# One written order for the transform units over all 376 steps, and B units on 128 rows

## The chip, the cores and the metric

The kernel runs on one core of a Trainium2 chip. The time is the device time in microseconds (us) of one execution; the time before is the median of three runs. Beside it there is one execution taken by the hardware profiler, whose instructions, queues and waits the profile page and the trace show. All durations below are from that execution.

## The reference, cut to what matters

```python
# x: (8, 3008, 256) float32; w_r, w_i: (256, 256); b_r, b_i: (256,)
X  = rfft(x, axis=1)
Yr = X.real @ w_r - X.imag @ w_i + b_r
Yi = X.real @ w_i + X.imag @ w_r + b_i
Yr, Yi = (sign(Y) * max(abs(Y) - 0.01, 0) for Y in (Yr, Yi))
y  = irfft(Yr + 1j * Yi, n=3008, axis=1)         # (8, 3008, 256)
h  = y.reshape(24064, 256) @ moe_w_in            # w_in: (256, 2048)
g  = where(h > 0, h, exp(min(h, 0)) - 1)         # ELU
out = g @ moe_w_out                              # w_out: (2048, 256), out: (24064, 256)
```

A Fourier transform along the sequence, a complex matrix product with a soft threshold in the frequency domain, the transform back, and then a two-layer network with ELU on each of the 24064 tokens.

## The kernel before

**The network** is cut into 376 steps. Tokens go in 47 blocks of 512, and each block takes eight steps; in step i, `front(i)` makes two 128-wide slices of h for one block (four matmuls with 512 columns, L1006; where the block crosses from one batch into the next each is split in two pieces), ScalarE takes the exponential, and a VectorE instruction (L1048, or L1050) joins it with h into `gT`. `back(i - 2)` multiplies the `gT` of two steps before with w_out (eight matmuls with 256 columns, L1080) into the sums of the block. Every eighth step the sums are copied to `osb` and stored.

The result of `front` lies in PSUM in a pool `psH` of two buffers, so `front(i + 1)` can begin only when the VectorE instruction of step i - 1 has read its `hps`. That instruction is put on VectorE by `finish_elu()` in the step after its own, behind whatever that step's unit puts on VectorE. A step has one of three ways to make the ELU:

- "pool": ScalarE makes two exponentials of 128x512, GpSimd a minimum and maximum of each (L1059), VectorE two instructions of 128x512.
- "act": ScalarE makes a ReLU and an exponential of 128x1024 (L1024, L1025), VectorE one instruction of 128x1024; GpSimd does nothing.
- otherwise: one exponential, then two VectorE instructions of 128x1024 (L1061, L1050). The first batch's steps use it.

**The transform** is cut into units, each put ahead of a step's `front`, so that TensorE does it between the step's matmuls. One batch has 6 units A (first stage of the transform, then a store to DRAM), 8 units X (second stage, after `load_Z` has brought the first one back from DRAM with its axes turned), 12 units M (`unit_M(b, q, i)`, the complex product with bias and threshold), 6 units B (`unit_B(b, q)`, first stage back, from the two M units of one q, then a store to DRAM) and 8 units Y (`unit_Y`, second stage back, after `load_Bs` has brought the B units' result back). Y units 0 and 1 make the first quarter of a batch's tokens, 2 and 3 the second, and so on.

A unit M makes six matmuls with 256 columns (L289, from batch 2 on; from the sum `XS` of real and imaginary part, made on GpSimd by `sum_XT`, L224). VectorE copies one product (L144) and adds it to the others (L296); GpSimd adds the bias (L301), clips (L302) and subtracts (L303) into the tile `Y`. A unit B takes `Y` as it lies, 64 rows for each of two halves s, with the real and the imaginary part c added up in PSUM: two pp times two c times two s, eight matmuls on 64 rows with 256 columns (L375).

The units share one PSUM buffer of two banks, or for M two buffers of one bank in the same place. `XT` and `Z` have one buffer each.

**The order** was made for each batch of 47 steps by `plan(b)`: M units stood in runs of two, three or four with a Y or B unit between the runs, and the X units of a batch came after the first Y units of the batch before. Steps with a unit M and a few more were in "act", other steps with units in "pool". Y units in an "act" step are read out by VectorE (L144), else by ScalarE (L146). The two Y units 0 and 1 of the next batch, "n" in the plan, stood at the end.

SyncE's queue carries, in the program's order, the loads and stores of A, X and B and the stores of the output; GpSimd's queue carries the loads of x. An instruction that waits holds up what is behind it on its queue.

The last lines of `unit_B` and the call of `finish_elu` in the loop are what the change and the steps below turn on:

```python
        for pp in range(2):
            for c in range(2):
                for s in range(2):
                    nc.tensor.matmul(
                        ps[:, s, pp * D : pp * D + D],
                        lhsT=M3[s * N2 : s * N2 + N2, 2 * v + pp, c, :],
                        rhs=Y[s * N2 : s * N2 + N2, pp, c * D : c * D + D],
```

Of the kernel before, what the change touches and what calls it, by code (L numbers as in the profile page):

```python
# [20 lines left out]
N2 = 64  # L21
# [8 lines left out]
def kernel(  # L30
# [28 lines left out]
    M3 = constp.tile([P, K1 // 2, 2, P], BF16, name="M3")  # L59
# [6 lines left out]
    bias_p = constp.tile([P, 2 * D], BF16, name="bias_p")  # L66
# [10 lines left out]
    space = constp.tile([P, 384], BF16, name="space")  # L77
# [26 lines left out]
    Y_of = {}  # L104
    Bz_of = {}
# [122 lines left out]
    def sum_of(dt, ch):  # L228

        return XS[:, 3 * dt + ch] if 3 * dt + ch < 5 else busy[:]  # L230

# [8 lines left out]
    def m_group(b, q, i, ps, biased=False):  # L240
# [10 lines left out]
        if i == 0:  # L251
            Y_of[b, q] = wk3.tile([P, 2, 2 * D], BF16, name="Y", tag="Y")
# [11 lines left out]
    def unit_M(b, q, i):  # L264
# [8 lines left out]
        if i == 0:  # L273
            Y_of[b, q] = wk3.tile([P, 2, 2 * D], BF16, name="Y", tag="Y")
# [10 lines left out]
        if o == 0 and b > 3:  # L285
            todo.append(todo.pop(0))
# [76 lines left out]

    def unit_B(b, v, alone=False, on_dve=False, all_dve=False):
# [5 lines left out]
        Bz, Y = Bz_of[b, v // 2], Y_of.pop((b, v))  # L370
        ps = unit_ps("bps", alone)
        for pp in range(2):
            for c in range(2):
                for s in range(2):
                    nc.tensor.matmul(  # L375
                        ps[:, s, pp * D : pp * D + D],
                        lhsT=M3[s * N2 : s * N2 + N2, 2 * v + pp, c, :],
                        rhs=Y[s * N2 : s * N2 + N2, pp, c * D : c * D + D],
                        start=(c == 0), stop=(c == 1),
                    )  # L380
# [33 lines left out]
    def split_B(v, ps, on_dve=(False, True), by_half=False):  # L414
# [8 lines left out]
        def half(pp):  # L423
            for c in range(2):
                for s in range(2):
                    nc.tensor.matmul(
                        ps[s][:, pp * D : pp * D + D],
                        lhsT=M3[s * N2 : s * N2 + N2, 2 * v + pp, c, :],
                        rhs=Y[s * N2 : s * N2 + N2, pp, c * D : c * D + D],
                        start=(c == 0), stop=(c == 1),  # L430
                    )
# [22 lines left out]
    def turn_B(v, ts=(0, 1), ps=None, on_dve=False):  # L454
# [11 lines left out]
        for pp in range(2):  # L466
            for dt in ts:
                for c in range(2):
                    for s in range(2):
# [7 lines left out]
                            rhs=M3[s * N2 : s * N2 + N2, 2 * v + pp, c, :].rearrange(  # L477
# [76 lines left out]

    nc.vector.memset(bias_p[:], 0.0)
# [274 lines left out]
    XS = sump.tile([P, 5, 512], BF16, name="XS")  # L830
# [60 lines left out]
    for o, src, sc, bi in ((1, w3, TURN, 0.0), (0, a3, -TURN, hpi[:])):  # L891
        if o == 0:
            nc.scalar.activation(a3[:], w3[:], AF.Abs)
        nc.scalar.activation(
            M3[:, :, 0, o * N2 : o * N2 + N2], src[:], AF.Sin, bias=bi, scale=sc
        )
# [3 lines left out]
        M3[:, :, 1, 0:N2], M3[:, :, 0, N2:P], 2.0, sgb, ALU.mult, ALU.mult  # L900
    )
    nc.vector.scalar_tensor_tensor(
        M3[:, :, 1, N2:P], M3[:, :, 0, 0:N2], -2.0, sgb, ALU.mult, ALU.mult
# [150 lines left out]
    def elu(i, hps, Et, on_pool, on_act):  # L1054
# [7 lines left out]
        late_elu.append((i, hps, Et, on_pool or on_act, on_pool))  # L1062
# [44 lines left out]
    def put(kind, b, *a):  # L1107
        return ({"A": unit_A, "X": unit_X, "M": unit_M, "B": unit_B, "Y": unit_Y}[kind], (b, *a))

    def plan(b):  # L1110

        f0 = [[] for _ in range(PER)]
        f1 = [[] for _ in range(PER)]
        mode = [None] * PER
        n1, n2 = b + 1, b + 2
        mid = [("X", u) for u in range(8)] + [
# [4 lines left out]
        ]  # L1121
        if n1 < B:
            if b:
                lead, xs = 0, (3, 6, 9) if b < 3 else (3, 8, 13)

                def M(q):
                    return [("M", q, 0), ("M", q, 1)]

                shift = b - 1 if b < 3 else b - 3
                seq = [("y", 2), ("y", 3)] + [None] * shift + [("X", u) for u in range(8)]  # L1130
                if b < 3:
                    seq += [("y", 4)] + M(0) + M(1) + [("y", 5), ("B", 0)]
                else:
                    seq += M(0) + [("y", 4)] + M(1) + [("y", 5), ("B", 0)]
                seq += M(2) + [("y", 6), ("B", 1)] + M(3) + [("y", 7), ("B", 2)]
                on_act = [("X", 4), ("X", 7), ("B", 3)] + [("y", u) for u in range(5, 8)]
                if b < 3:
                    on_act += [("A", 0)]
                    seq += M(4) + [("B", 3)] + M(5) + [("A", 0), ("B", 4), ("B", 5)]
                    seq += [("A", u) for u in range(1, 6)]  # L1140
                else:
                    on_act += [("y", 4), ("B", 4)]
                    seq += M(4) + [("B", 3), ("A", 0)] + M(5) + [("B", 4), ("A", 1), ("B", 5)]
                    seq += [("A", u) for u in range(2, 6)] + [None] * (3 if n2 == B else 2)
                seq += [("n", 0), ("n", 1)]
            else:
                lead, seq = FILL, (
                    [u for u in mid if u[0] != "A"]
                    + [("A", 0), ("A", 1), ("A", 2), ("n", 0), ("n", 1)]
                    + [("A", u) for u in range(3, 6)]  # L1150
                )
                xs = (12, 15, 18)
        else:
            lead, seq = 0, [("y", u) for u in range(2, 8)]
        for t, u in enumerate(seq, lead):
            if u is None:
                continue
            if b and n1 < B:
                mode[t] = "act" if u in on_act or u[0] == "M" else "pool"
            if mode[t] == "act" and u[0] != "M":  # L1160
                k = {"y": "Y"}.get(u[0], u[0])
                c = {"y": b, "A": n2}.get(u[0], n1)
                if c < B:
                    dve = (False, True) if k == "B" else (k != "X" or b < 3 and u[1] == 7,)
                    f0[t].append(put(k, c, u[1], False, *dve))
            elif u[0] == "y":
                f0[t].append(put("Y", b, u[1]))
            elif u[0] == "n":
                f0[t].append(put("Y", n1, u[1]))
            elif u[0] == "A":  # L1170
                if n2 < B:
                    f0[t].append(put("A", n2, u[1]))
            else:
                f0[t].append(put(u[0], n1, *u[1:]))
            if u == ("B", 5):
                f1[t + (b > 0 and n2 < B)] += [
                    (load_Bs, (n1, w, 0, 4 * K1 - 16 * (b == w == 0))) for w in range(4)
                ]
            if u == ("A", 5) and n2 < B:
                cuts = (0, 8, NS) if b else (0, 8, 16, 24, NS)  # L1180
                f1[t] += [(load_Z, (n2, *part)) for part in zip(cuts, cuts[1:])]
        if b == 0:
            for t in range(6):
                f1[t].append((unit_A, (1, t, False, t not in (0, 2), True)))
            for t, a, u in (
                (7, f0, 2), (7, f1, 3), (8, f0, 4), (8, f1, 5), (9, f0, 6), (9, f1, 7)
            ):
                a[t].append((split_Y, (0, u)))
            f1[1].insert(0, (scale_w_in, (1, True, 1)))
            for w in range(1, 4):  # L1190
                f1[w].append((load_Bs, (0, w)))
            f1[5] += [(load_Z, (1, s0, s1)) for s0, s1 in ((0, 8), (8, 16), (16, NS))]
            f1[xs[0]].append((lambda: gate(Z_of[1][:, 16, 0:1]), ()))
        if n2 < B:
            for ci in range(3):
                f1[xs[ci]].append((load_x, (n2, ci)))
        if b and n1 < B:
            f0[seq.index(("X", 4))].append((sum_XT, (n1, 0)))
            f0[seq.index(("X", 7))].append((sum_XT, (n1, 1, range(2 if b < 3 else 3))))
            if b < 3:  # L1200
                f0[seq.index(("M", 2, 0))].insert(0, (sum_XT, (n1, 1, (2,))))
        return f0, f1, mode

    f0 = f1 = None
    bare = 0
    early_h = None
    for i in range(n + LAG):
# [11 lines left out]
        elif i < n:  # L1219
            r = i % PER  # L1220
            if r == 0:
                f0, f1, mode = plan(i // PER)
                used = [bool(u0 or u1) for u0, u1 in zip(f0, f1)]
            free = not used[r]
            bare = bare + 1 if free else 0
            calm = free and (i >= n - 2 or (r + 2 < PER and not used[r + 1] and not used[r + 2]))
            for f, a in f0[r]:
                f(*a)
# [60 lines left out]
```

## Time and profile before

| | |
|---|---|
| time, median of three runs | 893.57 us (893.43 to 893.65) |
| span of the profiled execution | 903.9 us, from its first to its last instruction |
| TensorE busy | 891.3 us (99%) |
| VectorE, ScalarE, GpSimd busy | 679.6, 722.4, 596.7 us |
| granted TensorE clock | 0.948 on the mean; 0.95 in each of the stretches of 100 us from 100 to 800 us |
| units B (L375) | 336 matmuls on 64 rows, 42 units |
| DMA engines' share, 100 to 700 us | 0.39 to 0.42 |

A step is read in the timeline as the time from the first matmul behind one `back` to the first matmul behind the next. By what stands in the step its median is:

| step with | number | median us |
|---|---|---|
| no unit | 91 | 1.844 |
| X | 56 | 2.187 |
| Y | 56 | 2.194 |
| A | 36 | 2.314 |
| B | 42 | 2.396 |
| M (six matmuls of 256 columns) | 72 | 2.523 |
| M of batch 1 (four matmuls of 512) | 12 | 2.753 |

The steps that are over their median by more than 0.05 us are together 10.9 us over, from the 20th step to the last; 1.2 us of it lies in the first batch's part. Of the profiled execution's own time only the span of 903.9 us is known, 10.3 us above the median of the runs, which are timed without the profiler.

### The profile page before, as it was taken

The page shows a single profiled execution, that of the slowest core. Times are in us where ns is not written, and L with a number is a line of the kernel's source. Part 1 is how long each engine was busy: PE and PEld are TensorE (multiplying, and loading weights), DVE is VectorE, ACT ScalarE, POOL GpSimd, SP SyncE. Part 2 cuts the span into 40 slices and gives each one's busy share as a digit, 9 for nine tenths or more (in the row PEclk, how much of TensorE's full clock was granted, in tenths as well). Part 3 has the DMA queues.
Part 4 walks back from the last instruction along what each step waited for, and adds up shares of the span by engine and source line. Part 5 has one row for each costly group of instructions (what it writes and reads, how often), then busy time and mean ns, then how long its engine had stood idle before and what let it go on. Part 6 is the DMA issues. An engine that isn't in the chain of part 4 may idle for free.

```text
span 903.9 us, 18292 instructions
## 1 busy us (share of the span) xinstructions
PE 891.3 (99%) x6917; PEld 675.2 (75%) x6917; DVE 679.6 (75%) x969; ACT 722.4 (80%) x1001; POOL 596.7 (66%) x806
## 2 busy tenths in 40 slices
PE   9999999999999999999999999999999999999997
PEld 3467667877788777877778777787777877777776
DVE  7788778688866887668866788677876678778776
ACT  6778778888978889798887988878887798776654
POOL 7562550788657886588756877559875697753664
PEclk9999999999999999999999999999999999999998
DMA  8996226631474115632265231643218201241111
GB/s 262 310 258 188 70 71 181 169 119 47 118 209 124 65 50 152 173 117 88 72 181 136 86 116 48 189 140 101 87 53 229 70 24 48 69 108 36 28 44 47
DMA packets 90718, 105.85 MB, mean 117 GB/s; under 512 B 5395, under 2 KB 81174, under 8 KB 87302
## 3 DMA queue, kind: packets, MB, share of 16 engines
q1 hardware_dynamic: 84278, 76.64, 30.0%
q0 software_dynamic: 5968, 27.26, 9.4%
q8 instruction: 54, 0.88, 0.4%
q10 hardware_dynamic: 384, 0.79, 0.3%
q14 instruction: 34, 0.28, 0.1%
HBM read 54.86 MB, written 49.81 MB: 116 GB/s over the span
## 4 chain that ended last, share of the span: by engine, by line
PE 90%; DVE 3%; DMA 3%; ACT 2%; POOL 1%; issue 1%; SPq 0%; DVEq 0%; ACTq 0%; POOLq 0%
PE ps_o L1080 37%; PE hps L1006 36%; PE mps L289 5%; PE bps L375 2%; PE xps L207 2%; PE yps L538 2%; PE aps L170 2%; DVE gT L1048 2%; PE mps L247 1%; DVE Bz L144 1%; DMA xt<-in_x_dram 1%; DMA Z<-DA 1%; DMA DB<-Bz 1%; PE sps L1006 1%; DMA DA<-A 0%
## 5 line engine op out<-in xcount | busy, mean ns | idle before, releaser
L1048 DVE SCALAR_TENSOR_TENSOR gT<-Et,hps 128x512 fp32r<-128x512 f32 (+1 forms) x544 | 423.7, 811 | 158.5 <-POOL Et L1059 115.4
L1080 PE MATMUL ps_o<-w_out_r,gT 128*128 128x256 f32 x3008 | 481.4, 303 | 0.0
L1080 PEld LDWEIGHTS ps_o<-w_out_r,gT 128*128 128x128 f32 x3008 | 407.7, 190 | 52.4 <-ACT osb L1092 0.5
L1059 POOL TENSOR_SCALAR Et<-Et 128x512 f32<-128x512 f32 x434 | 258.3, 614 | 223.6 <-ACT Et L1022 213.2
L1006 PE MATMUL hps<-yT,w_in_s 128*128 128x512 bf16 (+7 forms) x1688 | 388.9, 360 | 2.0 <-DVE gT L1048 1.3
L1022 ACT ACTIVATE Et<-hps 128x512 f32<-128x512 f32 x412 | 224.2, 598 | 67.8 <-PE hps L1006 63.3
L1006 PEld LDWEIGHTS <-w_in_s 128*128 128x128 bf16 x1728 | 144.7, 99 | 119.7 <-issue 21.7
L1024 ACT ACTIVATE Et<-hps 128x1024 f32<-128x1024 f32 x130 | 133.6, 1027 | 57.3 <-PE hps L1006 49.0
L1025 ACT ACTIVATE Et<-Et 128x1024 f32<-128x1024 f32 x130 | 137.4, 1057 | 4.1
L301 POOL TENSOR_TENSOR yb<-yb,bias_bc 128x512 f32<-128x512 f32 x72 | 92.3, 1282 | 9.5 <-DVE yb L296 9.4
L303 POOL TENSOR_TENSOR Y<-yb,clip 128x512 bf16<-128x512 f32 x72 | 92.6, 1286 | 6.0
L296 DVE TENSOR_TENSOR yb<-mps,yb 128x512 f32<-128x512 f32 x72 | 49.8, 692 | 7.6 <-PE hps L1006 0.5
L146 ACT CAST XT<-xps 128x768 bf16<-128x768 f32 x57 | 45.5, 799 | 9.8 <-PE xps L207 9.7
L146 ACT CAST A<-aps 128x1024 bf16<-128x1024 f32 x40 | 40.5, 1014 | 11.4 <-PE aps L170 9.9
L302 POOL TENSOR_SCALAR clip<-yb 128x512 f32<-128x512 f32 x72 | 44.2, 614 | 6.3
L289 PE MATMUL mps<-wcat_s,XT 128*128 128x256 bf16 x288 | 44.1, 277 | 0.0
L144 DVE COPY yb<-mps 128x256 f32<-128x256 f32 x72 | 30.3, 421 | 11.1 <-PE mps L289 9.7
L1050 DVE SCALAR_TENSOR_TENSOR gT<-hps,Et 128x1024 fp32r<-128x1024 f32 x29 | 35.5, 1223 | 2.4
L224 POOL TENSOR_TENSOR XS<-XT 128x512 bf16<-128x512 bf16 x30 | 34.1, 1159 | 2.1 <-ACT XT L146 1.2
L1092 DVE COPY osb<-ps_o 128x512 f32<-128x512 f32 x46 | 31.6, 686 | 1.2 <-PE ps_o L1080 0.5
L146 ACT CAST Bz<-bps 128x1024 bf16<-128x1024 f32 x32 | 31.9, 998 | 0.5 <-PE bps L375 0.4
L1027 ACT ACTIVATE Et<-hps 128x1024 f32<-128x1024 f32 x29 | 29.8, 1029 | 2.6 <-PE hps L1006 1.2
(184 smaller groups left out, 678.8 us busy)
## 6 DMA issues: line engine op xcount, KB each, us to landing
xt<-in_x_dram POOLq DMA_DIRECT2D x21, 1024.0 KB, 5.4
out_dram<-osb SPq DMA_DIRECT2D x158, 128.0 KB
Bs<-DB SPq DMA_DIRECT2D x30, 384.0 KB
DB<-Bz SPq DMA_DIRECT2D x20, 512.0 KB
DA<-A SPq DMA_DIRECT2D x19, 512.0 KB
Z<-DA SPq DMA_DIRECT2D x5, 1152.0 KB
Z<-DA SPq DMA_DIRECT2D x11, 384.0 KB
xt<-in_x_dram POOLq DMA_DIRECT2D x6, 512.0 KB, 6.0
```

The costliest lines, as they stand in the source:

```text
L146: nc.scalar.copy(dst, src)
L289: nc.tensor.matmul(out_, lhsT=lhs[:, dt] if lhs is not None else sum_of(dt, ch)[:, oc : oc + P], rhs=w[:, dt, :], start=(dt == 0), stop=(d ...
L296: nc.vector.tensor_tensor(yb[:].rearrange("p (c d) -> p c d", c=2), ps[:].rearrange("p (c d) -> p c d", c=2), yb[:, D : 2 * D].unsqueeze(1 ...
L301: nc.gpsimd.tensor_tensor(yb[:], yb[:], bias_bc[:], ALU.add)
L303: nc.gpsimd.tensor_tensor(Y_of[b, q][:, i, :], yb[:], clip[:], ALU.subtract)
L1006: nc.tensor.matmul(hps[s][:, c0:c1] if early else hps[:, s, c0:c1], lhsT=w_in_s[:, dt, ft * P : ft * P + P], rhs=yT_of[b][:, dt, t0 : t0 + ...
L1022: nc.scalar.activation(E_[:, s], hps[:, s], AF.Exp)
L1024: nc.scalar.activation(E_, hps[:], AF.Relu, scale=-1.0)
L1025: nc.scalar.activation(E_, E_, AF.Exp, scale=-1.0)
L1048: nc.vector.scalar_tensor_tensor(o, e, -1.0, h, ALU.add, ALU.max)
L1059: nc.gpsimd.tensor_scalar(E_[s], E_[s], 1.0, 0.0, ALU.min, ALU.max)
L1080: nc.tensor.matmul(po[q][:, i_ % 2, :], lhsT=gT[:, s, i_ * P : i_ * P + P], rhs=w_out_r[:, ft, :], start=(ft == 0 and i_ % 2 == 0), stop=( ...
```

## The change

The order of the units is now written as text over steps 10 to 348 (`FIRST`, `SECOND`, `THIRD`, four times `STEADY`, `LAST`), and every batch from 4 on has the same 48 steps. M units stand three steps apart in `STEADY` (two in much of `SECOND`), X units of the next batch come ahead of the last B unit and of the Y units. A "-" is a step without a unit. Y units in `SECOND`, `THIRD` and `STEADY` are in a new way of the ELU, "join": exponentials and GpSimd as in "pool", the Y unit read out by VectorE, and one VectorE instruction of 128x1024. Steps with M are "act", all others there "pool". B units are no longer read out by VectorE.

Units B read `Yx`, a copy of `Y` with the real and the imaginary part of one half s on top of each other, 128 rows; `turn_Y` makes it with four DMAs on SyncE's queue in the step after the second M unit of a q. `M3x` is the matrix M3 laid out in the same way, made once in step 6. A unit B has four matmuls on 128 rows. M3 itself now shares its place with `XS` and with one `osb` buffer. The sums of `sum_XT` are spread over steps, the four loads of `load_Bs` too, and the matmuls from `XS` stand last in a batch's first unit M.

The diff, cut to its core:

```diff
-        if o == 0 and b > 3:
+        if o == 0:
             todo.append(todo.pop(0))
...
+    def by_part(dst, of):
+
+        for c in range(2):
+            for s in range(2):
+                nc.sync.dma_start(dst[c * N2 : c * N2 + N2, :, s, :], of(c, s))
+
+    def turn_M3():
+        by_part(M3x, lambda c, s: M3[c][s * N2 : s * N2 + N2])
+
+    def turn_Y(b, q):
+        Y = Y_of.pop((b, q))
+        Yx_of[b, q] = Yx = wk4.tile([P, 2, 2, D], BF16, name="Yx", tag="Y")
+        by_part(Yx, lambda c, s: Y[s * N2 : s * N2 + N2, :, c * D : c * D + D])
...
         for pp in range(2):
-            for c in range(2):
-                for s in range(2):
-                    nc.tensor.matmul(
-                        ps[:, s, pp * D : pp * D + D],
-                        lhsT=M3[s * N2 : s * N2 + N2, 2 * v + pp, c, :],
-                        rhs=Y[s * N2 : s * N2 + N2, pp, c * D : c * D + D],
-                        start=(c == 0), stop=(c == 1),
-                    )
+            for s in range(2):
+                nc.tensor.matmul(
+                    ps[:, s, pp * D : pp * D + D], lhsT=M3x[:, 2 * v + pp, s, :],
+                    rhs=Yx[:, pp, s, :], start=True, stop=True,
+                )
...
-    def elu(i, hps, Et, on_pool, on_act):
+    def elu(i, hps, Et, on_pool, on_act, joined):
...
-        late_elu.append((i, hps, Et, on_pool or on_act, on_pool))
+        late_elu.append((i, hps, Et, on_pool or on_act, on_pool and not joined))
...
+    def place(i, u, b):
...
+        if mode[i] == "join":
+            f0[i].append((unit_of[kind], (b, *a, False, True)))
+        else:
+            f0[i].append((unit_of[kind], (b, *a)))
+        if kind == "M" and a[1] == 1:
+            f1[i + 1].append((turn_Y, (b, a[0])))
+        if u == "B5":
+            for w in range(4):
+                f1[i + 1 + w].append((load_Bs, (b, w, 0, 4 * K1 - 16 * (b == 1 and w == 0))))
+        if u == "A5":
+            cuts = (0, 8, NS) if b > 2 else (0, 8, 16, 24, NS)
+            f1[i] += [(load_Z, (b, *part)) for part in zip(cuts, cuts[1:])]
+        if b > 1 and u == "X3":
+            for ch in range(3):
+                f1[i + 1 + ch].append((sum_XT, (b, 0, (ch,))))
+        if b > 1 and u == "X7":
+            for ch, k in enumerate((0, 2, 5)):
+                f1[i + k].append((sum_XT, (b, 1, (ch,))))
+
+    FIRST = """
+        X0 X1 X2 X3 X4 X5 X6 X7 M00 M01 M10 M11 M20 M21 B0 M30 M31 B1 M40 M41 B2 M50 M51
+        B3 A0 B4 B5 A1 A2 y0 y1 A3 A4 A5
+    """
+    SECOND = """
+        y2 y3 - X0 X1 X2 X3 X4 X5 X6 X7 M00 y4 M01 y5 M10 A0 M11 B0 M20 A1 M21 B1 M30 A2 M31
+        B2 M40 A3 M41 B3 M50 A4 M51 A5 y6 y7 B4 B5 - - X0 X1 y0
+    """
+    THIRD = """
+        y1 X2 X3 X4 X5 X6 X7 M00 y2 y4 M01 y3 M10 A0 y5 M11 B0 M20 A1 A2 M21 B1 M30 A3 A4 M31
+        B2 A5 M40 y6 B3 M41 y7 M50 - B4 M51
+        X0 X1 X2 X3 B5 X4 X5 X6 X7 - y0
+    """
+    STEADY = """
+        y1 y2 y3 M00 - y4 M01 - y5 M10 A0 B0 M11 A1 y6 M20 A2 B1 M21 A3 - M30 A4 B2 M31 y7 A5
+        M40 - B3 M41 - - M50 - B4 M51 X0 X1 X2 X3 B5 X4 X5 X6 X7 - y0
+    """
+    LAST = "y1 y2 y3 - - y4 - - y5 - - - - - y6 - - - - - y7"
...
+                    mode[at] = {"M": "act", "y": "join"}.get(u[0], "pool")
...
+        f1[6].append((turn_M3, ()))
```

`SECOND` begins at step 44, `THIRD` at 88, the `STEADY` parts at 136, 184, 232 and 280, `LAST` at 328. The units in all are the same as before: 72 M units of six matmuls, 42 B, 56 Y, 36 A.

175 lines of the change are left out of this document (62 added, 113 removed), and 4 rows, old and new, of the table mid.

## The prediction

> **What bounds the kernel now.** I read the page's busy times and its chain of waits first, then the timeline around single steps.
>
> ```profile
> PE 891.3 (99%) x6917; PEld 675.2 (75%) x6917; DVE 679.6 (75%) x969; ACT 722.4 (80%) x1001; POOL 596.7 (66%) x806
> ...
> PE 90%; DVE 3%; DMA 3%; ACT 2%; POOL 1%; issue 1%; SPq 0%; DVEq 0%; ACTq 0%; POOLq 0%
> ```
>
> TensorE (PE) is busy all the time and carries 90% of the chain. So only two things change the time: matmul time itself, and moments in which PE stands still. From the 20th step on these are 10.9 us (the steps over their medians, in the table above), so there is little to win. How much a unit B costs, the timeline shows:
>
> ```profile
> 457.06 0.62 PE L375 MATMUL bps<-Y,M 64*128 64x256 bf16 x8
> ...
> 457.61 1.06 PE L1006 MATMUL hps<-yT,w_in_s 128*128 128x512 bf16 x4
> ...
> 459.45 0.63 PE L170 MATMUL aps<-xt,M 128*128 128x512 f32 x2
> 459.92 1.06 PE L1006 MATMUL hps<-yT,w_in_s 128*128 128x512 bf16 x4
> ```
>
> The eight 64-row matmuls of a unit B hold PE from 457.06 to 457.61, 0.55 us; a unit A with 1024 columns 0.47 us. Eight times 256 columns one after the other would be twice as long as A: the two halves s already run side by side. Next, a unit M that follows a "pool" step (547.06 is its first matmul, 549.58 that of the next step):
>
> ```profile
> 547.06 0.28 PE L289 MATMUL mps<-wcat_r,XS 128*128 128x256 bf16 x1
> ...
> 547.49 0.42 DVE L144 COPY yb<-mps 128x256 f32<-128x256 f32 x1 [0.31 <-PE mps L289]
> ...
> 547.74 1.07 PE L1006 MATMUL hps<-yT,w_in_s 128*128 128x512 bf16 x4
> 548.02 0.69 DVE L296 TENSOR_TENSOR yb<-mps,yb 128x512 f32<-128x512 f32 x1
> ...
> 548.63 1.28 DVE L1048 SCALAR_TENSOR_TENSOR gT<-Et,hps 128x512 fp32r<-128x512 f32 x2
> 548.79 1.29 POOL L301 TENSOR_TENSOR yb<-yb,bias_bc 128x512 f32<-128x512 f32 x1 [0.19 <-DVE yb L296]
> ...
> 549.58 0.29 PE L289 MATMUL mps<-wcat_r,XS 128*128 128x256 bf16 x1
> ```
>
> VectorE (DVE) does the copy and the sum of M first, then the ELU of the step before, which ends at 549.91: 2.85 us after M began, while the M step itself takes 2.52. That ELU frees the `hps` buffer of the next `front`. Here nothing waits, since the next step begins with the 0.68 us of another M. Where a step has no such cover, it does wait:
>
> ```profile
> 772.15 1.22 DVE L144 CAST Bz<-bps 128x1024 bf16<-128x1024 f32 x1 [0.50 <-PE bps L375]
> ...
> 773.29 1.21 DVE L1048 SCALAR_TENSOR_TENSOR gT<-Et,hps 128x1024 fp32r<-128x1024 f32 x1
> ...
> 774.56 1.06 PE L1006 MATMUL hps<-yT,w_in_s 128*128 128x512 bf16 x4 [0.52 <-DVE gT L1048]
> ```
>
> This is a step without a unit behind a B read out by DVE: its `front` begins 0.06 us after the ELU's end (774.50), and the two steps took 0.67 us more than the median. Last, a unit Y read out by DVE, and a chain through DRAM on SyncE's queue:
>
> ```profile
> 515.14 0.51 PE L538 MATMUL yps<-M,Bs 96*128 96x94 bf16 x8
> ...
> 515.69 0.94 DVE L144 CAST yT<-yps 128x752 bf16<-128x752 f32 x1 [0.18 <-PE yps L538]
> ```
>
> ```profile
> 137.35 1.48 SPq L395 DMA_DIRECT2D DB<-Bz  x2
> 139.98 4.67 SPq L408 DMA_DIRECT2D Bs<-DB  x5
> ```
>
> `yT` is written 1.49 us after the unit's first matmul. A store of 256 KB was complete 2.63 us after its issue.
>
> **The change part by part**, in us of the profiled execution (span 903.9).
>
> *B units on 128 rows.* Four matmuls of 256 columns. Six of them take 0.68 in a unit M (547.06 to 547.74), so four take 0.45; 42 times (0.55 - 0.45) = -4.2.
>
> By the Trainium skill's page TensorEngine Tiling (Array Packing), sections Tiling Modes and Key Properties, 64-row tiles work in parallel and a change of the tiling mode drains TensorE. By that rule the regrouping wins no matmul time and only saves two drains per unit; the trace agrees, with 0.10 us for both.
>
> *What brings `Yx`.* 168 DMAs on SyncE's queue, by the five `Bs` loads (4.67 us with waits) and the two stores of 1.48 us below 0.8 us each, most near 0.37. The first waits for GpSimd's last instruction of the second M: GpSimd starts 1.73 after M's first matmul and needs 1.29 + 0.61 + 1.29 (L301 to L303), so it ends at 5.0; four issues to 6.5; complete by 9.1 with the 2.63 of the four times larger store. The B unit comes five steps after M, 10.6 to 12 us (four steps, 9.1, in one place). So 0; if a store of 512 KB stands ahead on the rings, up to 1 us at each of 42 units. Behind these waits on the queue stand output stores, which have eight steps, and the stores and loads of A, X and B, which mostly have eight or more.
>
> *Steps without a unit behind M* ("M01 -", "M40 -", "M41 -", "M50 -" four times, "M50 -" in `THIRD`). `front` can begin at 2.52, but the buffer is free at 2.85 + 0.06 = 2.91: 0.39 each, 17 times: +6.6. Behind "M41 - -" the second bare step needs M41's own ELU; ScalarE's ReLU starts 1.78 after M (548.84) and with the exponential ends at 3.9, the ELU at 5.16, `front` could start at 2.52 + 0.39 + 1.84 = 4.75: 0.46, four times: +1.8.
>
> *y1 in the step that needs it.* Blocks that begin at steps 88, 136, 184, 232, 280 and 328 cross into the next batch, and y1 stands in just these steps. `front`'s second matmul on the new batch waits for `yT` until 1.49 + 0.06 = 1.55 after y1 began, but is due at 0.35 plus the pieces ahead of it, 0.06 to 0.3; in step 328 ScalarE reads out, about 0.7 of waiting. Together 5.9. (Before, y1 stood at least one step earlier from batch 2 on.)
>
> *Y units in a row on DVE*: read-out 0.94 and ELU 1.22 are 2.16 of the 2.19 of a step, and the ELU that frees the next buffer stands behind the read-out. From y0 to the bare step behind M00 I walk: y1 0.28, y3 0.20 (an `osb` copy of 0.69 comes in between), M00 0.35, the bare step behind it 0.57; 1.4, four times: +5.6. In `SECOND` and `THIRD`: a bare step behind y3 0.57, a Y behind M00 (whose copy comes 0.3 later, as the `XS` products are last) 0.33 twice, pairs of Y units 0.25, 0.25, 0.12; +1.9.
>
> *GpSimd in `SECOND` and `THIRD`*: behind X7 it has a sum (1.17), M00's chain 3.2, a sum, a unit Y's two of 0.6, M01's chain within 9.4 us of PE. The Y unit's ELU comes late: 1.35 + 0.3 and 1.0, +2.7.
>
> *First batch*: y0 comes three steps (7.0 us) behind B5, before four (9.4). B5's store, then the `Bs` load behind the store of A1, are there after about 9: +2.0 (0 to 3). X0 comes four steps behind A5, before six: +0.5 (0 to 1.5).
>
> *Small waits* of 0.05 to 0.1 where A, B or X follow M: +2. *`turn_M3`* is due 24 steps in and starts behind `load_Z` near 70 us; the `osb` buffer that it reads from is next written in step 17: 0.
>
> *What goes*: all waits of before behind the first batch's part, 10.9 - 1.2 = -9.7, as every order in them is new.
>
> Sum: new waits 6.6 + 1.8 + 5.9 + 5.6 + 1.9 + 2.7 + 2.0 + 0.5 + 2.0 = 29.0; 29.0 - 4.2 - 9.7 = +15.1, 1.67% of 903.9, or 14.9 on the median of 893.57: 908.5. The granted clock is 0.95 throughout, even in the first 50 us with PE idle for a tenth, so waits don't buy clock.
>
> **The rivals.** *The order does its work* and its new waits don't arise: GpSimd's longest row, 3.2 us of each M against 2.52 per step in a run, is relieved at three steps, and the 9.7 go with the 4.2: 880; with a third of my new waits (9.7) 889. For it speaks that GpSimd's backlog disappears; against it that PE stands still for so little now, and that the buffer rule held at 774.56 to 0.06 us. It decides if the ELU behind an M ends by 2.5 us instead of 2.85. Chance 0.13. *Part of the new waits*, because one wait gives VectorE the time that the next would cost: two thirds of 29.0 are 19.3, 899; 896 to 903 have 0.15, and half of them, which is no change, 894, has 0.03. *`Yx` late*: SyncE's queue or rings hold `turn_Y` more than 2 us longer than I count; 0.5 to 1 us at 42 units on top, 925 to 950; for it that margins are 1.5 to 3 us, against it a DMA share of 0.4. Chance 0.09. *No change*: if 64-row matmuls ran one after the other, B would win 42 times 0.45 = 18.9 instead of 4.2 and cancel the rest, 894; the 0.55 speaks against it. Chance 0.02.
>
> **How the numbers follow.** The forecast has 0.58. Range: from 895, which takes in two thirds of the waits, to 921, with 3 for y0, 1.5 for X0 and some 10 us of late `Yx`. This leaves out the gain, 0.13, and most of late `Yx`. A measurement of this kernel tells 0.2% (1.8 us) from no change. Faster 0.13, same 0.05, slower 0.58 + 0.15 + 0.09 = 0.82.
>
> **What would show it.** Right: L1006 idle behind DVE's ELU line grows from 1.3 to over 8 us in PE's waits, with the first matmuls of bare steps behind M; PE's pieces in steps 136 to 280 wait for the Y read-out; the B group has 168 matmuls and unit steps of 2.30. Wrong: steps behind M at 1.84, or B units waiting for a DMA.

## The result and the profile after

The changed kernel takes 936.08 us (median of 4 runs, 931.62 to 936.83), before 893.61; the ratio estimated over all runs is 1.0461, 95% interval 1.0438 to 1.0484. The loss is 42.5 us; 14.9 were forecast. The direction was right, the size was not, and 936 lies outside the range.

```profile
span 934.7 us, 18351 instructions
...
PE 887.9 (95%) x6749; PEld 679.6 (73%) x6749; DVE 686.2 (73%) x979; ACT 669.2 (72%) x990; POOL 652.1 (70%) x898
...
PE 61%; DVE 11%; POOL 10%; DMA 8%; ACT 5%; issue 4%; SPq 1%; DVEq 0%; ACTq 0%; POOLq 0%
```

PE's share of the chain of waits fell from 90% to 61%; what came in is spread over VectorE, GpSimd, DMA and ScalarE, so no single wait makes the loss. PE's own waits (line, what it waited for, sum in us, times, longest), the first row before (first trace), the others after:

```profile
PE hps L1006 <- DVE gT L1048: 1.3, 3, 0.5
```

```profile
PE hps L1025 <- DVE gT L1067: 17.7, 43, 2.7
PE yps L555 <- DMA Bs<-DB: 5.2, 2, 3.1
PE hps L1025 <- DVE yT L146: 4.7, 6, 0.9
...
PE xps L209 <- DMA Z<-DA: 2.0, 2, 1.4
```

The wait of `front` (L1025) for the ELU (L1067) grew as forecast and to twice the size: from 1.3 to 17.7 us, forecast at over 8. Two waits for `Bs` of 5.2 us and those for `Z` were forecast at 2.5 together. For the size of each stretch a second trace of before was needed (first experiment), because the first one ran at a granted clock of 0.949 and this one at 0.996.

### The profile page after: what moved, and what is told of

Read it like the earlier page. It is cut to its first block, busy times and chain, and to the rows that moved or that the text cites. A ratio compares the mean times of both kernels' runs of the same rounds, so it can differ in the third digit from the quotient of the medians.

```text
span 934.7 us, 18351 instructions
## 1 busy us (share of the span) xinstructions
PE 887.9 (95%) x6749; PEld 679.6 (73%) x6749; DVE 686.2 (73%) x979; ACT 669.2 (72%) x990; POOL 652.1 (70%) x898
## 4 chain that ended last, share of the span: by engine, by line
PE 61%; DVE 11%; POOL 10%; DMA 8%; ACT 5%; issue 4%; SPq 1%; DVEq 0%; ACTq 0%; POOLq 0%
PE hps L1025 24%; PE ps_o L1099 24%; DVE gT L1067 5%; PE mps L295 3%; POOL Et L1078 3%; DMA Z<-DA 3%; POOL Y L309 2%; POOL yb L307 2%; PE bps L394 2%; PE mps L253 2%; POOL XS L226 2%; PE xps L209 2%; DVE yb L302 2%; PE yps L555 1%; ACT Et L1043 1%
## 5 line engine op out<-in xcount | busy, mean ns | idle before, releaser
L1067 DVE SCALAR_TENSOR_TENSOR gT<-Et,hps 128x512 fp32r<-128x512 f32 (+1 forms) x543 | 423.6, 812 | 167.7 <-POOL Et L1078 109.8
L1078 POOL TENSOR_SCALAR Et<-Et 128x512 f32<-128x512 f32 x526 | 313.1, 614 | 178.1 <-ACT Et L1041 164.6
L1025 PE MATMUL hps<-yT,w_in_s 128*128 128x512 bf16 (+7 forms) x1688 | 379.2, 351 | 25.6 <-DVE gT L1067 17.7
L1041 ACT ACTIVATE Et<-hps 128x512 f32<-128x512 f32 x504 | 274.9, 600 | 105.5 <-PE hps L1025 101.5
L1025 PEld LDWEIGHTS <-w_in_s 128*128 128x128 bf16 x1728 | 149.5, 98 | 138.5 <-issue 39.4
L1043 ACT ACTIVATE Et<-hps 128x1024 f32<-128x1024 f32 x84 | 86.3, 1028 | 99.1 <-PE hps L1025 99.1
L1044 ACT ACTIVATE Et<-Et 128x1024 f32<-128x1024 f32 x84 | 88.8, 1057 | 2.6
L146 DVE CAST yT<-yps 128x752 bf16<-128x752 f32 x47 | 44.2, 940 | 15.5 <-PE yps L555 15.3
L302 DVE TENSOR_TENSOR yb<-mps,yb 128x512 f32<-128x512 f32 x72 | 49.8, 692 | 7.8 <-DVE yb L146 0.9
L148 ACT CAST Bz<-bps 128x1024 bf16<-128x1024 f32 x42 | 42.6, 1014 | 7.5 <-PE bps L394 7.5
L555 PE MATMUL yps<-M,Bs 96*128 96x94 bf16 x448 | 28.8, 211 | 5.2 <-DMA Bs<-DB 5.2
```

The source lines that it names most:

```text
L146: nc.vector.tensor_copy(dst, src)
L148: nc.scalar.copy(dst, src)
L1025: nc.tensor.matmul(hps[s][:, c0:c1] if early else hps[:, s, c0:c1], lhsT=w_in_s[:, dt, ft * P : ft * P + P], rhs=yT_of[b][:, dt, t0 : t0 + ...
L1041: nc.scalar.activation(E_[:, s], hps[:, s], AF.Exp)
L1043: nc.scalar.activation(E_, hps[:], AF.Relu, scale=-1.0)
L1044: nc.scalar.activation(E_, E_, AF.Exp, scale=-1.0)
```

## The experiments

Below, a step lasts from its first matmul to the next step's, and its excess is what it takes over the usual step of its kind at full clock: 1.80 us bare, 2.48 M, 2.15 X and Y, 2.26 A; B 2.34 before and 2.26 after. So a wait ahead of a unit's first matmul counts to the step before: y0 of step 39 waits in step 38, X0 of step 47 in step 46, y0 of step 87 in step 86. All spans come from profiles, all other times are medians.

**Before, once more.**

> The kernel before, unchanged, for a second trace of it. Its first trace ran 903.9 us at a granted clock of 0.948, its timed runs 893.6. Theory A (the clock explains the gap, and my sum was made on a trace in which PE was slower than in the timed runs): a span near 892 comes with a clock near 0.996, and PE's idle time at its waits is then clearly over the 10.9 us that I counted from the 20th step on, some 20 us. Theory B (the clock has nothing to do with it): a span near 892 with a clock of 0.95, or 904 again at 0.996.

```profile
span 891.9 us, 18188 instructions
...
PE 873.7 (98%) x6813; PEld 669.1 (75%) x6917; DVE 680.4 (76%) x969; ACT 722.1 (81%) x1001; POOL 596.5 (67%) x806
...
PE 91%; DVE 4%; ACT 2%; issue 1%; POOL 1%; DMA 1%; DVEq 0%; ACTq 0%; POOLq 0%
```

894.12 us, span 891.9, clock 1.000. Theory A holds for the clock: a bare step takes 1.800 instead of 1.844, M 2.480 instead of 2.523. For the waits it holds in part: by the prediction's measure, over the median by more than 0.05, they are 15.0 us here against 10.9 in the first trace, not some 20, and almost the same steps carry them; with the steps above as the measure it is 16.5. So the sum was made on a trace 1.3% too slow, in which some 4 us of before's waits didn't show. The changed kernel has 58.5 us of excess in the same steps: 42.0 more, against 19.3 forecast (29.0 new less 9.7 that go). By stretch, in us, after against this trace:

| steps | before | after | excess, before | excess, after | more waiting | forecast |
|---|---|---|---|---|---|---|
| 10-43 `FIRST` | 82.7 | 85.0 | 1.4 | 4.2 | 2.8 | 2.5 |
| 44-135 `SECOND`, `THIRD` | 209.0 | 229.8 | 3.8 | 23.4 | 19.6 | about 4 |
| 136-327 `STEADY` | 432.6 | 445.3 | 10.7 | 28.4 | 17.7 | about 13 |
| 328-372 `LAST` | 83.4 | 85.9 | 0.4 | 2.5 | 2.1 | about 0.5 |
| from 373 to the end | 12.5 | 15.7 | | | 3.3 | 0 |

(Spans and waits differ by the B units, 0.1 us each, and by a few units that changed stretch.) The forecast column splits the prediction's terms by where they stand, its small waits and the waits that go shared out by the number of steps; X0's 0.5 is counted in `FIRST`, though its wait stands in step 46. Most of the miss is in `SECOND` and `THIRD`; `STEADY` is 4.7 over, and 3.3 come at the very end.

**The order alone.** B units on 64 rows straight from `Y`, as before; no `Yx`, no regrouped M3; all else as changed.

```diff
-  f1[i + 1].append((turn_Y, (b, a[0])))
-  matmul(ps[:, s, ...], lhsT=M3x[:, 2 * v + pp, s, :], rhs=Yx[:, pp, s, :])
+  for c in range(2): matmul(ps[:, s, ...], lhsT=M3[c][s * N2 : ..., 2 * v + pp, :], rhs=Y[...])
```

> The changed order with the B units as they were before (64-row operands straight from Y; no Yx, no regrouped M3). Theory A (the order's waits on VectorE and GpSimd make the loss): 42 units B cost about 0.09 us more each and nothing else changes, 936 + 3.6 = 938 to 941 us. Rival (the regrouping through SyncE's queue makes a good part of it): clearly under 930, down to 900 if it makes all of it.

935.86 us, between the two. The order makes the loss; the regrouping adds nothing in sum. But it does so by two parts that cancel: without `Yx`, `STEADY` is 3.4 us longer (24 B units at 64 rows), while `SECOND` and `THIRD` are 5.4 shorter, most of it because `Bs` for y0 of step 87 is there in time: 2.0 us of its wait, and 2.6 of the clock behind it (see the dummy matmuls below). In the changed kernel it isn't there:

```profile
254.30 2.53 SPq L1120 DMA_DIRECT2D out_dram<-osb  x4
256.93 0.55 SPq L417 DMA_DIRECT2D DB<-Bz  x1
262.31 1.72 SPq L425 DMA_DIRECT2D Bs<-DB  x4
```

```profile
266.23 0.51 PE L555 MATMUL yps<-M,Bs 96*128 96x94 bf16 x8 [2.06 <-DMA Bs<-DB]
```

SyncE's queue has four output stores, the store of the last B units, and 5.4 us later (forecast for such a store: 2.63) the `Bs` loads that wait for it; PE's row is y0, 2.06 us late. Behind the same four output stores the B store took 3.8 us without `Yx`. In the eight traces of the changed order that have `Yx`, no dummy matmuls and the ELU in its old place, the changed kernel's among them, it took 4.6 to 6.7, and y0 waited 1.1 to 2.1 us against 0.1. In the three with dummy matmuls, which also have `Yx`, it took 3.8 to 4.0, so how the DMAs of `Yx` delay the store isn't shown.

**The ELU ahead of the unit's read-out.**

```diff
+  if mode[i]:
+      finish_elu()
   for f, a in f0[i]:
       f(*a)
```

> The changed kernel with one difference: in every step from SECOND to the last STEADY the ELU of the step before is emitted ahead of the unit's read-out on VectorE, no longer behind it. Theory A (hps comes free late since the ELU stands behind the copy and sum of an M, or behind the read-out of a Y): the bare steps behind an M fall from 2.06-2.39 us towards 1.85 and the M steps behind a bare one from 2.9 towards 2.5; 915 to 928 us. Rival (the ELU isn't ready earlier, because its input from ScalarE or GpSimd comes late; then the unit's read-out stands behind it and GpSimd's chain starts later): 936 or more, up to 955.

1039.41 us, ratio 1.1611: both theories were far off. PE's waits name a third thing:

```profile
PE mps L295 <- DVE yT L146: 30.1, 21, 3.0
PE hps L1025 <- DVE gT L1067: 25.8, 48, 2.7
PE aps L172 <- DVE yb L302: 17.8, 18, 1.8
```

The units' PSUM tiles come free late when their read-out stands behind the ELU, and PE waits there instead: 103 us more, of which up to 12 are the clock's (seven stretches of 3.41 us at a granted clock of 0.50). VectorE has to serve `hps` and the units' tiles within one step; the order that the kernel has is the cheaper one.

**y1 needed last.** In the first step of a crossing block the matmuls go old batch, new batch `dt` 0, new batch `dt` 1.

```diff
+  if fp == 0 and crossing and not early:
+      todo.sort(key=lambda z: (z[2][0], z[3] if z[2][0] == new else 0))
```

> The changed kernel with one difference: in the first step of a block that crosses into the next batch, the matmuls are put in the order old batch, first half of the new batch's features, second half; so y1, which stands in that step, is needed last. Theory A (the step waits for y1's read-out): the six steps with y1 lose their 0.7 to 1.0 us each (step 88 more), 929 to 932 us. Rival (the wait only moves, because the same read-out and ELU on VectorE hold the next hps buffer): 934 to 937.

932.95 us, just above theory A. y1's step got 0.6 to 0.7 shorter at 88 and 136 (88: 2.62 us against 3.30 in the run with dummy matmuls below, which has no stretch at half clock there either) and 0.32 at 184: some 2.5 for six crossings. I had 5.9; the rest of those steps' excess stays when y1 isn't waited for, so by the order of the work it belongs to VectorE's row of Y units, which no run shows by itself.

**The regrouping alone.** The order of before, B units on 128 rows, the last B units one or two steps later (in the loop's first batch B0 to B3, by two).

```diff
-  M(5) + [("B", 4), ("A", 1), ("B", 5)]
+  M(5) + [("B", 4), ("A", 1), ("A", 2)] + [("B", 5)]
+  if u[0] == "M" and u[2] == 1: f1[t + 1].append((turn_Y, (n1, u[1])))
```

> The order of before with the regrouped B units of the change: 128-row matmuls, the four DMAs of Yx behind each second M, the four of M3x; the last B units of each batch stand one or two steps later, so that every B is at least four steps (three in the first batch) behind its M. Theory A (the regrouping is worth its matmul time and the DMAs cost little): 42 x 0.09 = 3.8 us less than before, 890 to 892 us. Rival (the DMAs delay the stores and loads around y0 and X0, as the run with 64-row units and the changed order suggests: there y0 of step 87 didn't wait): 895 to 903.

901.54 us, ratio 1.0086 (1.0066 to 1.0106): the rival.

```profile
PE bps L394 <- DMA Yx<-Y: 10.1, 14, 2.3
```

14 of 42 B units wait for `Yx`, 10.1 us; taken off, that leaves 891.4, an estimate that takes each wait to be worth its length. For B0 of one batch the chain reads: M01's first matmul at 509.68, first `Yx` DMA at 516.40 (6.7 later, 5.0 forecast, as GpSimd comes late), the four issues 2.6 us (1.5 forecast); B0 is due 12.3 us behind M01 and waits 0.9, so the chain took 13.2 instead of 9.1. The changed order has more room, and there B units wait for `Yx` 0.8 us in all.

**LAST's Y units in a row.**

```diff
-  LAST = "y1 y2 y3 - - y4 - - y5 - - - - - y6 - - - - - y7"
+  LAST = "y1 y2 y3 y4 y5 y6 y7"
```

> The changed kernel with LAST as y1 y2 y3 y4 y5 y6 y7, without the bare steps between them; so every step that takes the third hps buffer is also moved by one: 372 and not 374 is the last one. Theory A (PE's 2.70 us wait at 924.45 comes from the last two fronts taking the same third buffer one after the other, and the bare steps between the Y units cost 1.5 us): tail back by 2.7 to 3.4 us, another 1 to 1.5 from the Y units; 930 to 932.5. Rival (the wait at the end is the drain of the last block and stays, and Y units in a row cost what the bare ones did): 934.5 to 937.

928.82 us. `LAST` 85.9 to 84.7, the rest from step 373 on 15.7 to 12.5. In the changed kernel, just before the end:

```profile
923.11 1.28 DVE L1067 SCALAR_TENSOR_TENSOR gT<-Et,hps 128x512 fp32r<-128x512 f32 x2 [0.51 <-POOL Et L1078]
924.45 1.02 PE L1025 MATMUL hps<-yT,w_in_s 128*128 128x512 bf16 x4 [2.70 <-DVE gT L1067]
```

`third` picks every third step of a row of bare ones for the single third buffer (`fps`). With y7 in step 348 the last such step is 374, and the last `front` (375), which always takes that buffer, has to wait for its ELU. With y7 in step 334 it is 372, as before, and the same `front` starts without a gap:

```profile
913.22 1.90 PE L1025 MATMUL hps<-yT,w_in_s 128*128 128x512 bf16 x8
```

So 3.2 us of the loss come from a count modulo three. The rest of the 7.3 us may be the clock's (below): the four runs here have 0.997 to 0.999, not 0.996.

**GpSimd out of the Y units of `SECOND` and `THIRD`.**

```diff
-  mode[at] = {"M": "act", "y": "join"}.get(u[0], "pool")
+  y_mode = "act" if k < 3 else "join"
+  mode[at] = {"M": "act", "y": y_mode}.get(u[0], "pool")
```

> The changed kernel with the Y units of SECOND and THIRD in the mode of M (ReLU and exponential on ScalarE, nothing of the ELU on GpSimd), still read out by VectorE. Theory A (GpSimd's backlog of XS sums and M chains holds the ELU of the Y steps there, 2.6 us in steps 54 to 58 and 3.9 in steps 94 to 101): 929 to 932 us. Rival (VectorE's read-outs hold it, GpSimd is only the last to be seen): 935 to 938.

934.95 us, which looks like the rival, but the steps speak for A: excess 1.14 to 0.33 in step 58, 0.33 to 0.06 in 64, 1.15 to 0 in 98, 1.10 to 0.08 in 101; 3.3 us together. The gain is lost in step 38, whose wait for y0's `Bs` grew from 3.3 to 6.9 us:

```profile
138.71 0.60 POOL L119 DMA_DIRECT2D xt<-in_x_dram  x1 [9.15 <-PE aps L172]
```

With y2 and y3 off GpSimd, its queue reaches the 1 MB load of `xt`, which stands for step 46, at 138.71; in the changed kernel it gets there at 163.82. The load goes through the rings ahead of `Bs`: from 142 to 143 us they move 392 KB of it and nothing else.

**Output stores five steps later.**

```diff
-  q_.dma_start(ov[w, r0 : r0 + k // 8], osb[c0 : c0 + k, i_, :])
+  later.append((i, q_, ov[...], osb[...]))   # issued at step i + LAG + 5
```

> The changed kernel with the output stores issued five steps later, so that none stands directly ahead of the stores of B5 and A5 on SyncE's queue. Theory A (y0 and X0 of the first three batches wait for Bs and Z, 3.3 + 1.6 + 2.9 us, because the stores ahead of them share the rings with 0.5 MB of output; and the wait of 2.06 us at step 87 lets the granted clock fall to 0.50 for 6.8 us, which costs 3.4 more): 926 to 931 us, with no stretch of clock 0.50 before the tail. Rival (store, wait and load are slow by themselves): 934 to 938, with the same waits.

933.12 us, between the two. X0's wait in step 46 went from 1.6 to 0.9 and the 0.7 of step 49 to 0; y0's waits (3.6 in step 38, 1.9 in 86) stayed. In step 38 no output stood ahead of B5's store and the loads any more, so there it isn't what holds `Bs`. For step 86 the run doesn't tell: five output stores of an earlier block were issued from 253.37 on, and the B store right behind them at 257.06 took 6.7 us.

**STEADY's bare steps moved.** None behind an M; five between X7 and y0, three behind A.

```diff
-  y1 y2 y3 M00 - y4 M01 - y5 ... M40 - B3 M41 - - M50 - B4 M51 X0 X1 X2 X3 B5 X4 X5 X6 X7 - y0
+  y1 y2 y3 M00 y4 M01 y5 ... M40 B3 M41 M50 M51 X0 X1 B4 X2 X3 B5 X4 X5 X6 X7 - - - - - y0
```

> The changed kernel with STEADY's bare steps taken from behind the M units: no bare step follows an M any more, five stand between X7 and y0, three behind A units; B3 to B5 keep four steps or more from their M. Theory A (a bare step behind an M waits for its hps buffer until the ELU behind M's copy and sum is done): the four STEADY stretches lose the 0.4 us at M00, M01, M40, M41 and M50 and the 0.45 of the second bare step, about 2.5 each, 926 to 929 us. Rival (the wait goes on to the unit that now follows, since the ELU stays late whatever follows): 933 to 938.

934.26 us; the four `STEADY` stretches take 445.1 us against 445.3. The rival: the waits at M40, M41 and M50 are gone, and others of the same sum are there (excess of B4's step 1.34, of y5's 0.73, of A5's 0.61, of the first bare step behind X7 0.60).

**M's copy on ScalarE.**

```diff
-  evac(yb[:, D : 2 * D], k1[:, 0:D], True)
+  evac(yb[:, D : 2 * D], k1[:, 0:D], False)
```

> The changed kernel with the copy of an M's first 256 columns (0.42 us on VectorE) on ScalarE, which stands idle for about 1.2 us there. Theory A (the ELU behind M's two instructions on VectorE frees hps 0.33 to 0.45 us too late): the bare steps and units behind an M lose most of their 0.4, some 5 per STEADY, 925 to 931 us. Rival (ScalarE's ReLU and exponential of M's step come later by as much, and the next ELU waits for them; the wait moves by one step): 934 to 938.

933.45 us, below the rival's range, but in `STEADY` the M40, M41 and M50 steps are mostly 2.87 instead of 2.89 and the M01 steps 2.90 instead of 3.11 to 3.15; its four stretches are 1.0 us shorter together, next to nothing. The changed kernel's timeline around M40 (step 163) and the bare step behind it shows why theory A gains so little:

```profile
452.67 0.42 DVE L146 COPY yb<-mps 128x256 f32<-128x256 f32 x1
...
453.19 0.69 DVE L302 TENSOR_TENSOR yb<-mps,yb 128x512 f32<-128x512 f32 x1
...
453.80 1.27 DVE L1067 SCALAR_TENSOR_TENSOR gT<-Et,hps 128x512 fp32r<-128x512 f32 x2
...
455.13 1.02 PE L1025 MATMUL hps<-yT,w_in_s 128*128 128x512 bf16 x4 [0.33 <-DVE gT L1067]
```

The sum (L302) begins 0.1 us after the copy's end, but M's last matmul ends at 453.00: it is PE's matmuls that it waits for. The ELU behind it ends at 455.07 and the bare step's `front` starts 0.06 later, which is the buffer rule of the prediction.

**The store of A1 behind the `Bs` loads.**

```diff
+  elif (b, u) == (2, 1):
+      f1[40].append((nc.sync.dma_start, (dav[:, 0:8, :], A[:])))
```

> The changed kernel with one edit: the 512 KB store of A0 and A1 of the third batch is issued behind the four Bs loads of the second batch, not ahead of them. Theory A (those loads share the rings with that store, whose packets have 512 bytes): y0's wait of step 39 falls from 3.3 us to about 1, and no stretch of clock 0.50 follows there; 931 to 935. Rival (the wait is B5's own store and the four loads that start together): 3 us as before, 935 to 937.

933.13 us; step 38's excess falls from 3.3 to 1.6 and no stretch at half clock follows there, as in the changed kernel's trace. So half of that wait is the store ahead; the other half is left to B5's own store and the loads, which no run takes apart.

**TensorE kept busy while it waits.** Dummy matmuls into the tile that y0 overwrites.

```diff
+  for _ in range({1: 13, 2: 8}.get(b, 0) if u == 0 else 0):
+      nc.tensor.matmul(ps[:, 0, :], lhsT=busy[:, 0:P], rhs=busy[:], start=True, stop=True)
   for j in range(8):
```

> The changed kernel with one edit: 13 dummy matmuls (about 2.9 us) ahead of y0 of the second batch and 8 (1.8 us) ahead of y0 of the third, into the PSUM tile that y0 then overwrites, so that TensorE works while it waits for Bs. Theory A (a wait of 2 to 3 us is charged twice: by itself, and by a stretch of 3.4 or 6.8 us at a granted clock of 0.50 behind it): no such stretch before the tail, 931.5 to 933 us. Rival (the granted clock falls for another reason, or the dummies delay y0 more than they save): 936 or more.

930.58 us: theory A, and slightly more. The changed kernel's windows around y0 of step 87, then those of this run (columns: span; busy time and instructions of PE, PEld, DVE, ACT, POOL; granted clock; DMA share; GB/s):

```profile
262.00:264.00 2.00, 2.00 (x21) 1.59 (x18) 1.28 (x2) 1.74 (x4) 1.04 (x3) 1.00 0.31 57
264.00:267.00 3.00, 0.94 (x12) 0.54 (x11) 0.23 (x1) 0.37 (x1) 1.15 (x2) 1.00 1.00 295
267.00:274.00 7.00, 6.08 (x35) 5.15 (x33) 3.97 (x5) 2.17 (x4) 2.34 (x5) 0.54 0.79 234
274.00:278.00 4.00, 4.00 (x45) 3.48 (x45) 2.87 (x4) 3.08 (x6) 2.17 (x4) 0.95 0.00 0
```

```profile
262.00:267.00 5.00, 4.20 (x36) 2.80 (x35) 3.11 (x5) 1.09 (x2) 2.32 (x5) 1.00 0.76 182
267.00:274.00 7.00, 6.98 (x77) 6.13 (x77) 4.38 (x6) 5.46 (x10) 3.99 (x8) 1.00 0.60 185
```

After the wait of 2.06 us PE is granted half its clock from 267.6 to 274.4 and gets through 35 matmuls; in the same time the run with dummies, which is at other units by then, does 77. Half of 6.83 us would be 3.4, but steps 87 to 89 took 10.2 us here and 7.6 in each of four runs without the stretch (64-row B units, `LAST` in a row, M's copy on ScalarE, A1's store later): the stretch cost 2.6 us, still more than the wait. Three of the four runs with dummies have a clock of 1.000 (929.9 to 930.8 us); of the changed kernel's runs three have 0.996 (935.7 to 936.8), and one, by its clock of 0.999 without the stretch, took 931.62.

**Four edits together**, LAST in a row, Y units off GpSimd, y1 last (behind step 40), dummies:

> The changed kernel with four edits together: LAST's Y units in a row, the Y units of SECOND and THIRD in the mode of M, y1 needed last at the crossings behind step 40, and dummy matmuls ahead of y0 of the second and third batch (13 and 8, into the PSUM tile that y0 then overwrites), so that TensorE isn't idle while Bs comes. Theory A (they are separate losses): 4.4 + 3.7 + 2 + 3.4 us less, 921 to 924. Rival (one wait hides behind the other, they don't add): 926 to 930.

927.71 us: the rival, with step 39's wait for `Bs` at its longest, as `xt` goes first here too. The same with y2 and y3 of `SECOND` left on GpSimd:

```diff
-  y_mode = "act" if k < 3 else "join"
+  y_mode = "act" if k < 3 and at > 46 else "join"
```

> The four edits together once more, with one part taken back: y2 and y3 of SECOND stay on GpSimd. With them off GpSimd, its queue reached the 1 MB load of x early and that load stood in front of Bs (the wait of y0 in step 39 grew from 3.3 to 6.9 us). Theory A (that load is why the four didn't add up): 921 to 924 us, and the wait at y0 of step 39 back at 3 to 4 us. Rival (they don't add for another reason): 926 to 930.

923.32 us, theory A: the losses are separate, and `xt` was what hid it. 12.8 us of the 42.5 are recovered by four edits that touch neither the B units nor the order outside `LAST`.

**Two tries at a version better than both.** The order of before; the first six units B of the loop on 64 rows (a copy of M3's second half in a free `Bs` tile), 128 rows from the third batch on. First, each B about two steps later:

```diff
-  M(2) + [("y", 6), ("B", 1)] + M(3) + ...
+  M(2) + [("B", 0), ("y", 6)] + M(3) + [("B", 1), ("y", 7)] + M(4) + ...
```

> The order of before; from the third batch on 128-row B units, each some two steps later than before and five or more behind its second M; the first 6 units B in the loop stay on 64 rows, so no Yx is needed there. Theory A (what the regrouping costs is only the wait for Yx, 10.1 us in the run of the regrouping alone): 36 x 0.09 = 3.2 us less than before, 890 to 891.5. Rival (its DMAs or the later B units bring new waits): 893.5 to 898.

902.76 us, ratio 1.0093 (1.0078 to 1.0108), above what either theory had. No B waits for `Yx`; with B0 gone from between them, six M units stand in seven steps with 3.2 us of GpSimd each, and steps 67 and 115 are 2.8 and 3.3 us over, with `front` waiting up to 2.6 us for the ELU. Second, y6 in B0's place and B0 behind it:

```diff
-  M(1) + [("y", 5), ("B", 0)] + M(2) + [("y", 6), ("B", 1)]
+  M(1) + [("y", 5), ("y", 6), ("B", 0)] + M(2) + [("B", 1)]
```

> The order of before, 128-row B units from the third batch on, with y6 ahead of B0 and the last B of a batch one step later; M units stay in pairs of four with a Y or B between. Theory A (each B is now more than 12 us behind its second M, and no other wait is new): 36 x 0.09 = 3.2 us under before, 890 to 892. Rival (the Yx DMAs hold up SyncE's queue, or two Y units in a row cost VectorE what they cost in the changed order): 894 to 900.

895.21 us, ratio 1.0018 (1.0006 to 1.0030): the rival, narrowly. Its waits:

```profile
PE hps L1040 <- DVE gT L1082: 4.3, 16, 0.6
PE yps L570 <- DMA Bs<-DB: 1.5, 2, 0.9
PE bps L409 <- DMA Yx<-Y: 1.3, 3, 0.7
```

Over four batches it wins 1.4 us over before, and in steps 44 to 135 it loses 2.3: y0 waits twice for `Bs`, 1.5 us, and the second M behind B1 is twice 0.66 over, with `front` waiting for the ELU. Before stayed the fastest of all that ran.

## Why the prediction was right and wrong

*The B units* were right: -4.2 forecast; the median step of a B went from 2.364 to 2.267, 42 times is -4.1.

```profile
L375 PE MATMUL bps<-Y,M 64*128 64x256 bf16 x336 | 25.6, 272 | 0.2 <-ACT Bz L146 0.2
```

```profile
L394 PE MATMUL bps<-Yx,M3x 128*128 128x256 bf16 x168 | 25.9, 274 | 1.3 <-DMA Yx<-Y 0.8 <-ACT A L148 0.5
```

Half the matmuls with the same sum of busy time: that sum doesn't know that the 64-row ones ran two at a time. The step does.

*Bare steps behind M* were right in size: 0.39 forecast, 0.41 to 0.48 measured at M40, M41 and M50, 0.63 to 0.67 at M01 in three of its four places; 0.46 for the second bare step, 0.45 measured. Their number was too small: the last `STEADY` has no A and X units left, as they would belong to a ninth batch, and so six more bare steps stand behind an M there (at M10, M11, M20, M21, M30, M51), 0.35 to 0.55 each, 2.5 us. But as causes they were shown not to be separate: with the bare steps moved, the stretch took the same time. A sum of such waits may forecast a stretch; it doesn't say what taking one away brings.

*y1 and the row of Y units* were right in sum and wrong in their parts: 2.4 per batch forecast, 0.25 + 0.86 + 0.16 + 0.72 = 2.0 measured; y1 itself 0.3 to 0.7 instead of 1.0, by the run that needs it last.

*`SECOND` and `THIRD`* is the first step that failed: about 4 us net forecast, 19.6 measured. The prediction let `Bs` and `Z` be late for the first batch's units alone, 2.0 and 0.5, and gave the other stores and loads steps enough ("which mostly have eight or more"); y0 of step 87 stands five steps behind its B5. What was missing: `Bs` and `Z` later than their units (1.6 in step 46 and 0.7 in 49, against 0.5 forecast for X0; 2.2 in 86); the clock (2.6); units between two M units, six times 0.33 to 0.58 (3.1), which I had among 2 us of small waits for the whole kernel; and y7 in the very step, 80, that is the first to need it (1.0), the case that I priced for y1 and didn't look for elsewhere. The rest is spread over single steps. The GpSimd part, 2.7, held up: 3.3 went with the Y units' ELU off GpSimd. The 2.63 us for a store, taken from one place, fitted y0 of step 39 (2.5), where the loads behind it took longer; at step 87 the store took 5.4 with four output stores and `Yx` on the queue, and 3.8 without `Yx`.

*The end of the kernel* is the second: nothing forecast, 3.3 us measured, 2.7 of them one wait. `third` and its count modulo three stand in the kernel's loop, and the change moved where the count ends.

*The clock* is the third: "The granted clock is 0.95 throughout ... so waits don't buy clock". Not only was 0.95 particular to that one profile (1.000 in the second trace, and 0.998 to 1.000 in the ten runs beside it): a wait of 2 to 3 us can buy less clock. No wait of PE in before's loop is that long (the longest for the ELU is 0.5), so its trace could not show it; the sum had to be asked which of its own new waits would be. By the Trainium skill's page TensorE: Matmul & The Clock Gate, section What's actually happening, TensorE runs at half clock after an idle window of about 3.4 us until a busy one, and the windows run freely. The traces agree on the half clock and the grid: every stretch inside the loop lasts 3.41 or 6.83 us, and it comes in some runs only, as free windows would have it. They differ on the threshold that one would read from it: an idle stretch of 2.06 us was enough here, and one of 3.1 us at 143 us in the same run had no such stretch behind it.

*The rivals.* `Yx` late, at 0.09, was put in the wrong place: B units wait 0.8 us for it, but without `Yx` y0 of step 87 is 4.6 us cheaper, its clock stretch included; and in the order of before B units wait 10.1 us, more than the whole loss there. The 936 lies in that rival's range, but not by its cause. That the order does its work was refuted: with the B units as before it loses 42 us.

What stays open is the remainder: with the four edits 923.3 us, 29 over before. By the spans 14.6 of it lie in `SECOND` and `THIRD` and 11.4 in the four `STEADY` stretches, which also have the cheaper B units. The rows name VectorE's ELU behind M and Y, but that stays an argument: moving the bare steps or the copy recovered at most 1.0 us in `STEADY`, and moving the ELU cost 103.

## What to carry to other kernels

When an order is rewritten, price the ends of the chains through DRAM with what stands ahead of them on the queue, not with a quiet store's time, and look for every unit that lands in the first step that needs it. Ask of each new wait of TensorE whether it is longer than any that the trace has: a wait past 2 us can be charged a second time in clock. A buffer that is taken by a count modulo something is an edit of its own, wherever the count starts anew.

## What the hardware showed that was not expected

- The first trace of before has a granted clock of 0.949 from 7 to 901 us and a span of 903.9 us; the second, of the same kernel, has 1.000 and 891.9. A clock 5% lower cost 1.3%.
- Waits of PE of 2 to 3 us came with 3.41 or 6.83 us at a granted clock of 0.50, in some runs and not in others. The run of 931.62 us had none by its clock of 0.999; the other runs of the changed kernel took 4.1 to 5.2 us more, of which the one trace accounts for 2.6.
- Work taken from GpSimd in steps 44 and 45 let a transfer start 25 us early, and that delayed a load on SyncE's queue by 3.6 us in step 38; with the work put back the delay went.
